# An mLSTM layer with two dense layers behind it on one core: leaky relu twice on ScalarE, its remainder read from the bank, the weights' integer addition on VectorE, and new durations in the planner

## The chip, the cores and the metric

The kernel runs on one core of one Trainium2 chip. The metric is the device time of one execution in microseconds; before the change the median of three runs is 894.95 us (892.51 to 896.52). In the text PE is TensorE, DVE is VectorE, ACT is ScalarE, POOL is GpSimd and SP is SyncE, whose queue issues every DMA of this kernel. A "bank" is one 128x512 float32 buffer of PSUM.

## The reference

Inputs are q, k, v and an output gate of shape (4, 8, 768, 40), two gates per head and token, and float64 weights of two dense layers. The recurrence runs over 768 tokens; its output, 3072 tokens by 320 columns, goes through two dense layers with 2048 hidden columns.

```python
for t in range(S):
    m_new = np.maximum(f_gate[:, :, t] + m, i_gate[:, :, t])
    f_stab = np.exp(f_gate[:, :, t] + m - m_new)
    i_stab = np.exp(i_gate[:, :, t] - m_new)
    C = f_stab * C + i_stab * einsum(v_t, k_t)
    n = f_stab * n + i_stab * k_t
    y[:, :, t] = sigmoid(o_t) * (C q_t) / max(abs(n q_t), 1)
x = y.transpose(0, 2, 1, 3).reshape(B * S, H * D)
h = x @ w_in;   x = np.maximum(0.01 * h, h) @ w_out        # layer 0
h = np.maximum(x @ w_in2, 0.0);   out = (h * h) @ w_out2   # layer 1
```

## The kernel before

**Tiling.** The recurrence is cut into six chunks of 128 tokens. A block is the same chunk of all four batches, 512 tokens, and each layer handles six blocks of 16 hidden tiles of 128 columns. To keep float32 accuracy a product is split into high and low float32r parts: `moe_h` writes a hidden tile with 8 matmuls into one of two banks named hp (line 424), `out1` (lines 454 to 460) adds 8 matmuls per tile into three accumulator banks in layer 0, and `out2` (lines 502 to 504) does the same with 12 shorter matmuls in layer 1. Block 0 of layer 0 is worked in halves of 256 tokens, because its tiles can only start as the weights come in; all other blocks go 512 tokens at a time. Attention of chunk 2 to 5 runs beside blocks 1 to 4 of layer 0, and attention of chunk 1 beside block 0.

**From a hidden tile to its two parts, layer 0.** The tile in the bank hp goes through four instructions: ACT copies it times 0.01 into g (line 430), DVE takes the maximum of g and the bank (line 431), ACT rounds that to the high part gH (line 435), and g minus gH is the low part gL (line 436), on DVE, or in block 0 also on POOL. The bank is free again after line 431.

**Weights.** A piece of weights comes as 704 float64 numbers per partition. DVE shifts and masks the high word (line 384) and merges it (line 386), ACT scales the low word (line 388), POOL adds the two as integers (line 389), ACT rounds the sum to the high parts (line 391), and the low parts are subtracted on DVE or POOL (lines 395 and 400). There are 16 pieces per layer; those of layer 0 are converted during start-up and block 0, those of layer 1 from block 4 of layer 0 on.

**What sets the order.** The program's order on every engine is written by a list scheduler, the class `Sched`. Each operation has an engine, a duration in ns, a priority, and the buffers that it reads and writes; an operation with `alt` may go to a second engine if the plan finds it free earlier. The scheduler runs the plan forward, works back from it to new priorities, and keeps the best of six passes. While the plan has PE idle in the first microseconds it puts in matmuls on zeros (lines 312, 450, 467), called fillers below. On the chip each engine runs its list strictly in order and waits by semaphores. Durations come from small functions such as

```python
def mm(n, m=128):                 # one pass of a float32r product
    return max(m / 1.2, n / 2.4 + 2.5, 25)
def dve(n, two_x=False):
    return (n / (2 if two_x else 1) + 66) / 0.96
```

**DMA.** SP issues all transfers in the planned order. The split queries and keys of a chunk are spread over partitions by nine transfers per batch, `T<-X` (line 569), after a rounding on ACT (line 564) and a subtraction on DVE (line 565); the products of line 623 wait for them.

Of the kernel before, what the change touches and what calls it, by code (L numbers as in the profile page):

```python
# [30 lines left out]
ORDER = dict(pe0=7000, ld2=80, kv=-5.41, ks=6.4, g2=32.54, z=-8.14, lag=7, m0=0.71, o0=1.33, a04=-6.78, a0s=5.39, a1=30.61, a1s=6.5, a1ld=23.83, w0=-23.81, ws=2.43, bias=0.88, c0=-7.4, cs=11.88, cld=28.29, wl=1.51, outk=2.04)  # L31
PASSES = 6                # of the list scheduler
# [6 lines left out]
class Buf:  # L39
    def __init__(self, tag, make):  # L40
        self.tag, self.make, self.t = tag, make, None
        self.first, self.left, self.last_w, self.readers, self.live = None, 0, {}, {}, tag is None


class Node:
    __slots__ = ("eng", "dur", "fn", "key", "deps", "outs", "ndep", "ready", "allocs", "bufs", "end", "start", "table", "lat", "seq", "alt", "after", "first")


class Sched:
# [10 lines left out]
    def op(self, eng, dur, key, fn, r=(), w=(), table=None, lat=0, alt=None, after=0):  # L60
        """fn() emits; r and w are the (buffer, region) pairs that it reads and writes; alt: another
        engine that may take it instead, with its time and fn."""
# [22 lines left out]
        n.bufs = list(bufs.values())  # L85
        n.deps = list(deps.values())
# [5 lines left out]
    def order(self, passes):  # L92
        """The best of some passes; each after the first takes its priorities from the one before: when an
        operation has to start for TensorE's operations to keep their order and to follow one another."""
        import copy

        best = None
        for i in range(passes):
            try:
                plan, total = self.forward()  # L100
            except RuntimeError:
                if best is None:
                    raise
                break
            if best is None or total < best[1]:
                best = [copy.copy(n) for n in plan], total
            self.backward(plan, total)
        return best[0]

    def backward(self, plan, total):  # L110
# [5 lines left out]
        for n in sorted((n for n in plan if n.seq >= 0), key=lambda n: (n.start, n.seq), reverse=True):  # L116
# [8 lines left out]
            if n.eng == "PE":            # the latest free time  # L125
# [8 lines left out]
    def forward(self):  # L134
# [103 lines left out]
def mm(n, m=128):                 # one pass of a float32r product  # L238
    return max(m / 1.2, n / 2.4 + 2.5, 25)
# [15 lines left out]
def mlstm_moe_kernel(  # L255
# [70 lines left out]
    def gate_part(lo, hi, key):  # L326
# [11 lines left out]
        op("DVE", dve(n), key, lambda: V.tensor_tensor_scan(m1(), f(), i(), NEG if lo == 0 else mt.t[:, lo:lo + 1], ALU.add, ALU.max),  # L338
# [11 lines left out]
        op("DVE", dve(n), key, lambda: V.tensor_tensor_scan(f(), am.t[:, 1, o], a(), 0.0, ALU.mult, ALU.add), r=[AA, (am, "mask")], w=[F])  # L350
# [5 lines left out]
        if lo:  # L356
            op("SP", 570, key + 0.1, lambda: SP.dma_start(out=Adram.t[:, o], in_=G_sb.t[32:64, o]), r=[(G_sb, f"A{p}")], w=[(Adram, p)], lat=500)
# [5 lines left out]
    wt, fs = {}, {}  # L363

    def weight(layer, j, key):
# [11 lines left out]
        op("SP", 570, key - 20, lambda: SP.dma_start(out=raw.t, in_=wts[layer, j].bitcast(I32).rearrange("p (n w) -> p n w", w=2)), w=[(raw, 0)], lat=2200)  # L377
# [11 lines left out]
        op("POOL", pool(WR), key, lambda: G.tensor_tensor(out=ft(), in0=ft(), in1=l.t, op=ALU.add), r=[(fb, fr), (l, 0)], w=[(fb, fr)])  # L389
# [7 lines left out]
        # the last 64 rows of w_in: its high parts in partitions 0..63, its low parts in 64..127  # L397
# [41 lines left out]

    def out1(c, lo, n, j, key):  # L440
# [7 lines left out]
        if j == 0 and n < BLK and lo == 0:      # one group of the whole bank for both halves  # L448
# [41 lines left out]
    def out2(c, j, key):  # L490
# [5 lines left out]
        for b in range(B):  # L496
# [10 lines left out]
            if last:  # L507
# [335 lines left out]
```

## Time and profile before

| quantity | value |
|---|---|
| three runs | 892.51, 896.52, 894.95 us; median 894.95 |
| profiled execution | span 888.7 us from the first to the last instruction; its time as a run is not listed beside it |
| busy in the span | PE 849.6, DVE 593.7, ACT 472.6, POOL 181.8 us |
| mean granted clock of TensorE | 0.975 |
| end of block 0 of layer 0 (line 472) | 167.1 us |
| ends of blocks 1, 2, 3 | 246.0, 325.9, 407.6 us |
| end of layer 0 | 541.5 us |

Busy shares are means over stages with different limits, so the stages are read apart below. The span is 6.3 us below the median of the runs, and differences are carried over to the median as they are.

### The profile page before, as it was taken

The page shows a single profiled execution, that of the slowest core. Times are in us where ns is not written, and L with a number is a line of the kernel's source. Part 1 is how long each engine was busy: PE and PEld are TensorE (multiplying, and loading weights), DVE is VectorE, ACT ScalarE, POOL GpSimd, SP SyncE. Part 2 cuts the span into 40 slices and gives each one's busy share as a digit, 9 for nine tenths or more (in the row PEclk, how much of TensorE's full clock was granted, in tenths as well). Part 3 has the DMA queues.
Part 4 walks back from the last instruction along what each step waited for, and adds up shares of the span by engine and source line. Part 5 has one row for each costly group of instructions (what it writes and reads, how often), then busy time and mean ns, then how long its engine had stood idle before and what let it go on. Part 6 is the DMA issues. An engine that isn't in the chain of part 4 may idle for free.

```text
span 888.7 us, 14153 instructions
## 1 busy us (share of the span) xinstructions
PE 849.6 (96%) x5244; PEld 732.1 (82%) x5244; DVE 593.7 (67%) x1047; ACT 472.6 (53%) x946; POOL 181.8 (20%) x190
## 2 busy tenths in 40 slices
PE   7988789999999999999999999999999999999998
PEld 5777789877777777777777888889999999999997
DVE  6699996877787778776867789964353443433433
ACT  5457665964775496558546556543343433433332
POOL 3387771511322042001000332200000000000000
PEclk8589899999999999999999999999999999999999
DMA  8477445434533444443331333200000000000000
GB/s 226 151 237 235 140 143 176 157 113 128 157 123 125 129 140 138 134 156 107 87 116 33 127 116 112 71 1 30 1 30 1 1 30 1 23 8 1 30 1 30
DMA packets 55992, 83.62 MB, mean 94 GB/s; under 512 B 4756, under 2 KB 44404, under 8 KB 55924
## 3 DMA queue, kind: packets, MB, share of 16 engines
q1 hardware_dynamic: 55924, 82.73, 29.2%
q8 instruction: 41, 0.67, 0.3%
q14 instruction: 27, 0.22, 0.1%
HBM read 54.43 MB, written 4.01 MB: 66 GB/s over the span
## 4 chain that ended last, share of the span: by engine, by line
PE 58%; DVE 17%; SPq 9%; DMA 6%; ACT 4%; issue 3%; POOL 3%; DVEq 0%; POOLq 0%; ACTq 0%
PE hp L424 25%; SPq L569 8%; DMA T<-X 4%; PE acc L503 3%; PE acc L504 3%; PE acc L502 3%; POOL qkr L389 2%; DVE gL L436 2%; PE acc L454 2%; DVE w L395 2%; PE acc L456 2%; PE acc L455 2%; PE attS L623 2%; PE atty L633 1%; DVE g L431 1%
## 5 line engine op out<-in xcount | busy, mean ns | idle before, releaser
L424 PE MATMUL hp<-xH,w 128*128 128x512 f32 (+1 forms) x1040 | 297.2, 383 | 8.1 <-DVE g L431 6.4
L424 PEld LDWEIGHTS hp<-xH,w 128*128 128x128 f32 x1040 | 185.8, 192 | 37.9 <-DVE g L431 7.1
L424 PE MATMUL hp<-xL,w 128*128 128x512 f32 (+1 forms) x624 | 201.4, 379 | 0.0
L436 DVE TENSOR_TENSOR gL<-g,gH 128x512 fp32r<-128x512 f32 (+1 forms) x196 | 143.3, 732 | 68.5 <-ACT gH L435 68.2
L435 ACT CAST gH<-g 128x512 fp32r<-128x512 f32 (+1 forms) x208 | 121.9, 586 | 124.6 <-DVE g L434 73.7
L434 DVE TENSOR_TENSOR g<-g 128x512 f32<-128x512 f32 x96 | 72.9, 759 | 114.2 <-ACT g L433 114.2
L424 PEld LDWEIGHTS hp<-xL,w 128*128 128x128 f32 x624 | 116.6, 191 | 22.9
L433 ACT ACTIVATE g<-hp 128x512 f32<-128x512 f32 x96 | 57.4, 598 | 122.4 <-PE hp L424 122.4
L431 DVE TENSOR_TENSOR g<-g,hp 128x512 f32<-128x512 f32 (+1 forms) x112 | 67.6, 605 | 29.9 <-ACT g L430 28.6
L456 PE MATMUL acc<-gL,w 128*128 128x512 f32 (+1 forms) x224 | 82.2, 367 | 4.7 <-DVE gL L436 2.4
L430 ACT ACTIVATE g<-hp 128x512 f32<-128x512 f32 (+1 forms) x112 | 59.7, 534 | 49.3 <-PE hp L424 41.2
L454 PE MATMUL acc<-gH,w 128*128 128x512 f32 (+1 forms) x224 | 85.9, 384 | 0.0
L455 PE MATMUL acc<-gH,w 128*128 128x512 f32 (+1 forms) x224 | 81.3, 363 | 0.0
L617 POOL TENSOR_SCALAR_AFFINE_SELECT aw<-aw 128x512 f32<-128x512 f32 x48 | 36.1, 754 | 118.2 <-ACT aw L614 117.8
L503 PE MATMUL acc<-w,gH 128*128 128x320 f32 x192 | 59.4, 309 | 0.0
L504 PE MATMUL acc<-w,gL 128*128 128x320 f32 x192 | 59.3, 309 | 0.0
L502 PE MATMUL acc<-w,gH 128*128 128x320 f32 x192 | 59.2, 308 | 0.0
L614 ACT ACTIVATE aw<-aw,cs 128x128 f32<-128x128 f32 x160 | 51.1, 392 | 5.0 <-DMA aw<-Adram 4.9
L456 PEld LDWEIGHTS acc<-gL,w 128*128 128x128 f32 x224 | 42.9, 192 | 12.6 <-POOL gL L436 2.7
L389 POOL TENSOR_TENSOR qkr<-qkr,wl 128x704 int32<-128x704 int32 x16 | 30.5, 1909 | 100.1 <-DVE qkr L386 60.6
L455 PEld LDWEIGHTS acc<-gH,w 128*128 128x128 f32 x224 | 43.1, 192 | 5.7
L454 PEld LDWEIGHTS acc<-gH,w 128*128 128x128 f32 x224 | 43.2, 193 | 5.4
(162 smaller groups left out, 1569.9 us busy)
## 6 DMA issues: line engine op xcount, KB each, us to landing
T<-X SPq DMA_DIRECT2D x180, 120.0 KB
x<-in_wts_dram SPq DMA_DIRECT2D x16, 704.0 KB
aw<-Adram SPq DMA_DIRECT2D x40, 256.0 KB
nat<-in_nat_dram SPq DMA_DIRECT2D x24, 328.0 KB
qkr<-in_qk_dram SPq DMA_DIRECT2D x20, 360.0 KB
X<-in_wts_dram SPq DMA_DIRECT2D x8, 704.0 KB
T<-in_wts_dram SPq DMA_DIRECT2D x8, 704.0 KB
og<-in_og_dram SPq DMA_DIRECT2D x12, 320.0 KB
```

Source lines behind the costliest of these rows:

```text
L424: T.matmul(hp.t[:, 0:n], w.t[:, col:col + 128], x.t[:, kt, o], start=(s == 0), stop=(s == 7))
L431: op("DVE", dve(n), key, lambda: V.tensor_tensor(out=g.t[:, 0:n], in0=g.t[:, 0:n], in1=hp.t[:, 0:n], op=ALU.max), r=[(hp, 0), (g, 0)], w=[ ...
L434: op("DVE", dve(n), key, lambda: V.tensor_tensor(out=g.t[:, 0:n], in0=g.t[:, 0:n], in1=g.t[:, 0:n], op=ALU.mult), r=[(g, 0)], w=[(g, 0)])
L435: op("ACT", act(n), key, lambda: A.copy(gH.t[:, 0:n], g.t[:, 0:n]), r=[(g, 0)], w=[(gH, 0)])
L436: lo_ = lambda eng: eng.tensor_tensor(out=gL.t[:, 0:n], in0=g.t[:, 0:n], in1=gH.t[:, 0:n].bitcast(F32), op=ALU.subtract)
L454: T.matmul(a[t].t[:, o], w.t[:, hc:hc + 128], gH.t[:, 0:n], start=first, stop=False)
L455: T.matmul(a[t].t[:, o], w.t[:, lc:lc + 128], gH.t[:, 0:n], start=False, stop=False)
L456: T.matmul(a[t].t[:, o], w.t[:, hc:hc + 128], gL.t[:, 0:n], start=False, stop=last)
L502: T.matmul(a.t[:, 0:DM], gH.t[:, s], wH, start=first, stop=False)
L503: T.matmul(a.t[:, 0:DM], gH.t[:, s], wL, start=False, stop=False)
L504: T.matmul(a.t[:, 0:DM], gL.t[:, s], wH, start=False, stop=last)
L569: op("SP", 570, kx, lambda tt=tt, X=X, blk=blk, r=r, x0=x0, x1=x1: SP.dma_start(out=tt.t[blk * D:(blk + 1) * D, :, r].bitcast(F32), in_=X. ...
```

## The change

The comments were also taken out of the file, so that line numbers shift by 7 to 9 (line 430 becomes 438, 436 becomes 440, 389 becomes 396).

```diff
         if layer == 0:
-            op("ACT", act(n, True), key, lambda: A.activation(g.t[:, 0:n], hp.t[:, 0:n], AF.Copy, scale=0.01), r=[(hp, 0)], w=[(g, 0)])
-            op("DVE", dve(n), key, lambda: V.tensor_tensor(out=g.t[:, 0:n], in0=g.t[:, 0:n], in1=hp.t[:, 0:n], op=ALU.max), r=[(hp, 0), (g, 0)], w=[(g, 0)])
+            h = lambda: hp.t[:, 0:n]
+            op("ACT", act(n, True), key, lambda: A.activation(gH.t[:, 0:n], h(), AF.Prelu, alpha=0.01), r=[(hp, 0)], w=[(gH, 0)])
+            op("ACT", act(n, True), key, lambda: A.activation(h(), h(), AF.Prelu, alpha=0.01), r=[(hp, 0)], w=[(hp, 0)])
+            op("DVE", dve(n), key, lambda: V.tensor_tensor(out=gL.t[:, 0:n], in0=h(), in1=gH.t[:, 0:n].bitcast(F32), op=ALU.subtract), r=[(hp, 0), (gH, 0)], w=[(gL, 0)])
...
-        op("ACT", act(n), key, lambda: A.copy(gH.t[:, 0:n], g.t[:, 0:n]), r=[(g, 0)], w=[(gH, 0)])
-        lo_ = lambda eng: eng.tensor_tensor(out=gL.t[:, 0:n], in0=g.t[:, 0:n], in1=gH.t[:, 0:n].bitcast(F32), op=ALU.subtract)
-        op("DVE", dve(n), key, lambda: lo_(V), r=[(g, 0), (gH, 0)], w=[(gL, 0)], alt=("POOL", pool(n), lambda: lo_(G)) if n < BLK else None)
...
-        op("POOL", pool(WR), key, lambda: G.tensor_tensor(out=ft(), in0=ft(), in1=l.t, op=ALU.add), r=[(fb, fr), (l, 0)], w=[(fb, fr)])
+        add = lambda eng: eng.tensor_tensor(out=ft(), in0=ft(), in1=l.t, op=ALU.add)
+        op("DVE", dve(WR), key, lambda: add(V), r=[(fb, fr), (l, 0)], w=[(fb, fr)], alt=("POOL", pool(WR), lambda: add(G)))
...
-def mm(n, m=128):
-    return max(m / 1.2, n / 2.4 + 2.5, 25)
+def mm(n):
+    return max(112, 0.4427 * n + 5.6)
...
+                b = busy[{"DVE": "POOL", "POOL": "DVE"}.get(e)] if e in ("DVE", "POOL") else None
+                if b and not n.bank and not b.bank:
+                    dur += SHARE * min(dur, max(0, b.start + b.dur - now))
```

With `SHARE = 0.6` the plan lengthens an operation of DVE or POOL that starts while the other of the two is busy, unless one of them touches a bank (`n.bank`). Other durations in the plan change as well: a DMA issue from 570 to 420 ns, and to 800 for the transfers `T<-X` and the copies of the state; the two scans of the gates, the transposes, and the small products of attention. The priorities in the table `ORDER` stay as they were. In layer 1 the four instructions per tile stay.

Since the plan changes, the order changes on all engines; three places follow. The first is DVE at the start, behind the first part of the gates. `T`, `x_0` and `x_1` belong to the gates' scans, `x_2` and `x_4` to the first piece of weights, and `aw` times `attS` is the first product of attention, which PE waits for. Before:

```order
L338 SCALAR_TENSOR_TENSOR T<-x_0_73,T 32x128
L340 TENSOR_TENSOR x_1_82<-x_0_73,T 32x128
L338 SCALAR_TENSOR_TENSOR T<-x_0_73,T 32x512
L341 TENSOR_TENSOR x_1_82<-x_1_82,T 32x128
L340 TENSOR_TENSOR x_1_82<-x_0_73,T 32x512
L349 TENSOR_TENSOR x_0_73<-x_0_73,T 32x512
L341 TENSOR_TENSOR x_1_82<-x_1_82,T 32x512
L344 TENSOR_SCALAR x_1_82<-x_1_82 32x128
L344 TENSOR_SCALAR x_1_82<-x_1_82 32x512
L349 TENSOR_TENSOR x_0_73<-x_0_73,T 32x128
L626 TENSOR_TENSOR aw<-aw,attS 128x512
```

Now:

```order
L345 SCALAR_TENSOR_TENSOR T<-x_0_73,T 32x128
L635 TENSOR_TENSOR aw<-aw,attS 128x512
L635 TENSOR_TENSOR aw<-aw,acc_163 128x512
L345 SCALAR_TENSOR_TENSOR T<-x_0_73,T 32x512
L391 TENSOR_SCALAR x_2_226<-x_4_125 128x704
L347 TENSOR_TENSOR x_1_82<-x_0_73,T 32x512
```

The two products moved ahead of nine gate operations. On SP the second load of the gates, for which the first of these rows waits, stands tenth instead of seventh.

The second place is in block 0, one or two pieces of weights on DVE, around the eighth piece. Before:

```order
L384 TENSOR_SCALAR x_2_254<-x_4_586 128x704
L565 TENSOR_TENSOR X<-qkr,X 120x2x384
L386 SCALAR_TENSOR_TENSOR x_2_254<-x_4_586,x_2_254 128x704
L740 TENSOR_TENSOR xL<-attm,xH 128x3x128
L431 TENSOR_TENSOR g<-g,hp 128x256
L626 TENSOR_TENSOR aw<-aw,attS 128x512
L384 TENSOR_SCALAR x_3_278<-x_5_636 128x704
L431 TENSOR_TENSOR g<-g,hp 128x256
L386 SCALAR_TENSOR_TENSOR x_3_278<-x_5_636,x_3_278 128x704
L395 TENSOR_TENSOR w_878<-x_2_254,w_878 128x512
```

Now:

```order
L391 TENSOR_SCALAR x_2_226<-x_4_657 128x704
L440 TENSOR_TENSOR gL<-hp,gH 128x256
L393 SCALAR_TENSOR_TENSOR x_2_226<-x_4_657,x_2_226 128x704
L635 TENSOR_TENSOR aw<-aw,attS 128x512
L749 TENSOR_TENSOR xL<-attm,xH 128x3x128
L396 ISA x_2_226<-x_2_226,wl 128x1408
L391 TENSOR_SCALAR x_3_354<-x_5_667 128x704
L440 TENSOR_TENSOR gL<-hp,gH 128x256
L393 SCALAR_TENSOR_TENSOR x_3_354<-x_5_667,x_3_354 128x704
L403 TENSOR_TENSOR w_880<-x_2_226,w_880 128x512
```

The maximum (L431) is gone, the remainder (L440) has its place and reads the bank, and the integer addition (L396) has come in as an instruction of its own kind whose row speaks of 1408 elements. Of the 16 additions of layer 0, ten are on DVE and six on POOL; of layer 1's, fifteen and one. All 32 remainders of half tiles are on DVE (before 20, and 12 on POOL). Of the 16 small subtractions of line 400 (now 408) in layer 0 none is on DVE (before four), and of the 512-wide ones of line 395 (now 403) thirteen are (before fifteen).

The third place is ACT in a later block of layer 0. Before:

```order
L430 ACTIVATE g<-hp 128x512
L657 CAST x_5_1933<-aw 128x512
L435 CAST gH<-g 128x512
L729 COPY y<-y 128x64
L430 ACTIVATE g<-hp 128x512
L739 CAST xH<-attm 128x3x128
L435 CAST gH<-g 128x512
```

Now:

```order
L438 ACTIVATE gH<-hp 128x512
L738 COPY y<-y 128x64
L439 ACTIVATE hp<-hp 128x512
L748 CAST xH<-attm 128x3x128
L438 ACTIVATE gH<-hp 128x512
L439 ACTIVATE hp<-hp 128x512
```

Each tile still has two ACT instructions, and both now read the bank; the second writes it. The number of table loads on ACT is the same in both programs. Of the fillers, fifteen of line 467 (now 476) stand in the order instead of ten, and as many as before of the two other lines.

## Rows read from the trace of the kernel before

**Rows 1.** Windows by stage: us, busy (instructions) per engine, granted clock, DMA.

```profile
0.00:44.00 44.00, 38.34 (x207) 29.53 (x208) 28.43 (x63) 21.40 (x49) 14.89 (x22) 0.69 0.62 189
44.00:133.00 89.00, 73.23 (x597) 69.09 (x596) 85.11 (x142) 57.40 (x133) 68.13 (x68) 0.90 0.59 188
133.00:167.00 34.00, 33.37 (x293) 31.51 (x292) 24.44 (x56) 22.98 (x56) 10.69 (x14) 1.00 0.59 176
167.00:541.50 374.50, 361.06 (x2250) 291.96 (x2249) 290.99 (x549) 236.79 (x483) 75.82 (x81) 1.00 0.38 121
541.50:888.70 347.20, 343.60 (x1905) 309.97 (x1903) 164.77 (x242) 134.07 (x228) 12.23 (x7) 1.00 0.06 20
```

**Rows 2.** Groups of DVE, 44 to 133 us: count, busy us, mean ns, idle before.

```profile
L386 DVE SCALAR_TENSOR_TENSOR x<-x,x 128x704 int32<-128x704 int32 x13 | 13.6, 1043 | 0.1
L395 DVE TENSOR_TENSOR w<-x,w 128x512 fp32r<-128x512 f32 x13 | 12.7, 974 | 0.1
L384 DVE TENSOR_SCALAR x<-x 128x704 int32<-128x704 int32 x12 | 10.3, 865 | 0.0
L436 DVE TENSOR_TENSOR gL<-g,gH 128x256 fp32r<-128x256 f32 x12 | 9.5, 806 | 0.5 <-ACT gH L435 0.5
L431 DVE TENSOR_TENSOR g<-g,hp 128x256 f32<-128x256 f32 x23 | 9.3, 412 | 0.5 <-ACT g L430 0.3
L400 DVE TENSOR_TENSOR w<-x,w 64x128 fp32r<-64x128 f32 x3 | 4.6, 1530 | 0.1
```

**Rows 3.** The same lines over the whole span: ns shortest/median/longest, starts, forms.

```profile
L386 DVE SCALAR_TENSOR_TENSOR x<-x,x x16: 874/884/1941, 25.2 to 122.4; 128x704 int32<-128x704 int32 x16
L395 DVE TENSOR_TENSOR w<-x,w x15: 676/834/2079, 34.5 to 127.7; 128x512 fp32r<-128x512 f32 x15
L384 DVE TENSOR_SCALAR x<-x x16: 511/522/1985, 22.3 to 120.4; 128x704 int32<-128x704 int32 x16
L436 DVE TENSOR_TENSOR gL<-g,gH x196: 409/692/1908, 55.1 to 881.0; 128x512 fp32r<-128x512 f32 x176, 128x256 fp32r<-128x256 f32 x20
L400 DVE TENSOR_TENSOR w<-x,w x4: 289/504/3581, 36.3 to 104.7; 64x128 fp32r<-64x128 f32 x4
```

**Rows 4.** Timeline of DVE and POOL around 96 us: start, length, what.

```profile
95.99 3.58 DVE L400 TENSOR_TENSOR w<-x,w 64x128 fp32r<-64x128 f32 x1
...
96.50 1.29 POOL L395 TENSOR_TENSOR w<-x,w 128x512 fp32r<-128x512 f32 x1
97.76 1.66 POOL L389 TENSOR_TENSOR x<-x,wl 128x704 int32<-128x704 int32 x1
```

**Rows 5.** Groups of POOL, 44 to 133 us.

```profile
L389 POOL TENSOR_TENSOR x<-x,wl 128x704 int32<-128x704 int32 x14 | 26.7, 1909 | 7.8 <-DVE x L386 7.7
L436 POOL TENSOR_TENSOR gL<-g,gH 128x256 fp32r<-128x256 f32 x10 | 11.5, 1147 | 2.2 <-ACT gH L435 2.0
L400 POOL TENSOR_TENSOR w<-x,w 64x128 fp32r<-64x128 f32 x11 | 8.1, 737 | 4.8 <-ACT w L391 2.3 <-issue 1.4 <-POOL aw L617 0.5
```

**Rows 6.** Waits of PE, 44 to 133 us, by releaser: us, times, longest.

```profile
PE hp L424 <- DVE g L431: 6.4, 2, 3.9
```

**Rows 7.** The line of ACT's first instruction per hidden tile, layer 0.

```profile
L430 ACT ACTIVATE g<-hp x112: 360/592/603, 48.5 to 533.4; 128x512 f32<-128x512 f32 x80, 128x256 f32<-128x256 f32 x32
```

**Rows 8.** Windows at the start, columns as in rows 1.

```profile
12.50:17.00 4.50, 0.18 (x2) 0.00 (x0) 4.50 (x10) 4.18 (x5) 1.52 (x2) 0.72 0.89 291
17.00:41.50 24.50, 24.41 (x118) 19.40 (x120) 16.26 (x34) 11.47 (x32) 10.07 (x11) 0.50 0.51 167
```

**Rows 9.** Groups of DVE, 167 to 541 us.

```profile
L436 DVE TENSOR_TENSOR gL<-g,gH 128x512 fp32r<-128x512 f32 x81 | 62.5, 772 | 10.5 <-ACT gH L435 10.4
L431 DVE TENSOR_TENSOR g<-g,hp 128x512 f32<-128x512 f32 x79 | 53.9, 682 | 26.3 <-ACT g L430 25.4
```

**Rows 10.** Waits of PE, 167 to 541 us.

```profile
PE attS L623 <- DMA T<-X: 8.3, 15, 0.7
```

**Rows 11.** SP's issues of those transfers.

```profile
L569 SPq DMA_DIRECT2D T<-X x180: 767/768/1244, 49.9 to 451.9; - x180
```

More of the change, by code (lines that the diff above doesn't have):

```diff
@@ L31 @@
 ORDER = dict(pe0=7000, ld2=80, kv=-5.41, ks=6.4, g2=32.54, z=-8.14, lag=7, m0=0.71, o0=1.33, a04=-6.78, a0s=5.39, a1=30.61, a1s=6.5, a1ld=23.83, w0=-23.81, ws=2.43, bias=0.88, c0=-7.4, cs=11.88, cld=28.29, wl=1.51, outk=2.04)
+SHARE = 0.6
 PASSES = 6
@@ L42, in __init__ @@
         self.first, self.left, self.last_w, self.readers, self.live = None, 0, {}, {}, tag is None
+        self.bank = False
 class Node:
-    __slots__ = ("eng", "dur", "fn", "key", "deps", "outs", "ndep", "ready", "allocs", "bufs", "end", "start", "table", "lat", "seq", "alt", "after", "first")
+    __slots__ = ("eng", "dur", "fn", "key", "deps", "outs", "ndep", "ready", "allocs", "bufs", "end", "start", "table", "lat", "seq", "alt", "after", "first", "bank")
 class Sched:
@@ L85, in op @@
         n.bufs = list(bufs.values())
+        n.bank = any(b.bank for b in n.bufs)
         n.deps = list(deps.values())
@@ L282, in ps @@
         b = sc.buf(tag, None, 2 if tag == "hp" else 1)
+        b.bank = True
         b.make = lambda: pp.tile([128, 512], F32, tag=tag, name=tag, bufs=sc.slots[tag])
@@ L301, in mlstm_moe_kernel @@
     for lo, hi in ((0, CH), (CH, S)):
-        op("SP", 570, -1000, lambda lo=lo, hi=hi: SP.dma_start(out=fi.t[:, :, lo:hi], in_=gates[:, :, lo:hi].rearrange("g p s -> p g s")),
+        op("SP", 420, -1000, lambda lo=lo, hi=hi: SP.dma_start(out=fi.t[:, :, lo:hi], in_=gates[:, :, lo:hi].rearrange("g p s -> p g s")),
            w=[(fi, f"{x}{p}") for x in "fi" for p in ((0,) if lo == 0 else (1, 2))], lat=250)
@@ L337, in gate_part @@
         ck = lambda x: x.rearrange("p (k t) -> p k t", t=CH)
-        op("DVE", dve(n), key, lambda: V.tensor_tensor_scan(m1(), f(), i(), NEG if lo == 0 else mt.t[:, lo:lo + 1], ALU.add, ALU.max),
+        op("DVE", 3.4 * n, key, lambda: V.tensor_tensor_scan(m1(), f(), i(), NEG if lo == 0 else mt.t[:, lo:lo + 1], ALU.add, ALU.max),
            r=[F, I, (mt, p)], w=[(mt, p + 1)])
@@ L349, in gate_part @@
         op("DVE", dve(n), key + 0.1, lambda: V.tensor_tensor(out=i(), in0=i(), in1=m1(), op=ALU.subtract), r=[I, (mt, p + 1)], w=[I])
-        op("DVE", dve(n), key, lambda: V.tensor_tensor_scan(f(), am.t[:, 1, o], a(), 0.0, ALU.mult, ALU.add), r=[AA, (am, "mask")], w=[F])
+        op("DVE", 2.2 * n + 60, key, lambda: V.tensor_tensor_scan(f(), am.t[:, 1, o], a(), 0.0, ALU.mult, ALU.add), r=[AA, (am, "mask")], w=[F])
         op("DVE", dve(n, True), key, lambda: V.tensor_copy(G_sb.t[32:64, o], f()), r=[F], w=[(G_sb, f"A{p}")])
@@ L376, in weight @@
         wt[layer, j] = w
-        op("SP", 570, key - 20, lambda: SP.dma_start(out=raw.t, in_=wts[layer, j].bitcast(I32).rearrange("p (n w) -> p n w", w=2)), w=[(raw, 0)], lat=2200)
+        op("SP", 420, key - 20, lambda: SP.dma_start(out=raw.t, in_=wts[layer, j].bitcast(I32).rearrange("p (n w) -> p n w", w=2)), w=[(raw, 0)], lat=2200)
         l = sb("wl", [128, WR], I32, 2)
@@ L633, in mI @@
                             T.matmul(py.t[:, (8 + n) * E:(9 + n) * E], lhs(0, h), st, start=True, stop=True)
-                    op("PE", 4 * (214 if native else 107), key + 0.35, mI, r=tk + ([(C32, (b, 0)), (C32, (b, 1))] if native else [(Cst, (b, k)) for k in range(3)]), w=[(py, 0)])
+                    op("PE", 4 * (214 if native else 113), key + 0.35, mI, r=tk + ([(C32, (b, 0)), (C32, (b, 1))] if native else [(Cst, (b, k)) for k in range(3)]), w=[(py, 0)])
                 def mPV(py=py, aw=aw, v=v, hd=hd):
@@ L659, in attention @@
                        alt=("POOL", pool(512), lambda lw=lw: lw(G, 1)))
-                    op("PE", 4 * 145, key + 0.5, mPV3, r=[(pb, (pr, i)) for i in range(3)] + [(vb, (vr, i)) for i in range(3)], w=[(py, 0)])
+                    op("PE", 4 * 126, key + 0.5, mPV3, r=[(pb, (pr, i)) for i in range(3)] + [(vb, (vr, i)) for i in range(3)], w=[(py, 0)])
                 else:
@@ L693, in mU @@
                         T.matmul(up.t[r:r + D, o:o + E], nt.t[:, h * D:(h + 1) * D], wv.t[:, h], start=True, stop=True)
-                op("PE", 8 * 62, kU, mU, r=[(nt, 0), (wv, 0)], w=[(up, 0)])
+                op("PE", 730, kU, mU, r=[(nt, 0), (wv, 0)], w=[(up, 0)])
                 st = lambda b=b: C32.t[:, 8 * b:8 * b + 8]
@@ L734, in mT @@
                     T.transpose(xp.t[:, k * 128:(k + 1) * 128], y.t[:, k * 128:(k + 1) * 128], ident.t)
[L736 removed]
+            op("PE", 3 * 112, ko + 0.75, mT, r=[(y, 0), (y, 1), (ident, 0)], w=[(xp, 0)])
             xo = slice(b * CH, (b + 1) * CH)
```

33 lines of the change are left out of this document (17 added, 16 removed).

## Prediction

> **What bounds the kernel now.** I read the windows by stage first. In layer 1, the last 347 us, PE is busy 99% of the time at full clock [rows 1]; the change leaves its four instructions per tile as they are, so nothing is to be had there. Blocks 1 to 5 of layer 0 (167 to 541.5 us) have PE busy 361.1 of 374.5 us: 13.4 us idle. The stage to look at is 44 to 133 us, start of block 0: PE is busy only 73.2 of 89 us and gets a mean clock of 0.90, while DVE is busy 85.1 us, 96%, and POOL 68.1 us, 77%. DVE is the bound there. It converts the weights, serves attention and the hidden tiles, and the PE waits that are left in that stretch come from it, as the 6.4 us for line 431 do [rows 6]. From 133 to 167 us PE catches up, 98% busy.
>
> Second, what DVE does in that stretch. Its groups are longer than they need be: line 386 takes 1043 ns in the mean where its shortest takes 874, line 395 974 against 676, line 384 865 against 511, line 436 806 against 409, line 400 1530 against 289 [rows 2, 3]. Line 431 with 412 ns is not stretched: half of its input comes from a bank. The timeline shows how the others are. One subtraction of 64x128 elements on DVE starts at 95.99 us and lasts 3.58 us, 12 times its shortest, and ends when two POOL operations that started beside it have ended, at 97.79 and 99.42 us [rows 3, 4]. Summed over the five lines (13 x 169, 13 x 298, 12 x 354, 12 x 397 and 3 x 1241 ns) this stretching is 2.2 + 3.9 + 4.2 + 4.8 + 3.7 = 18.8 us.
>
> [...]
>
> **The change part by part.** The sum is made against the profiled span of 888.7 us, 6.3 us under the median of the runs, and carried to the median, 894.95.
>
> *Block 0, DVE's own work at shortest durations.* Removed: 32 maxima of half tiles at 0.412 = 13.2 us, and 20 remainders that DVE had at 0.409 = 8.2 us; four small subtractions and two wide ones go to POOL, 4 x 0.289 + 2 x 0.676 = 2.5 us. Added: 32 remainders that read the bank, the form of line 431, 32 x 0.412 = 13.2 us; and ten integer additions. No row shows such an addition on DVE. Below, I take line 384, which goes over the same 704 words with one source, 0.51 us; above, twice line 386, since the order speaks of 1408 elements, 1.75 us. I take line 386 itself, 0.88 us, nearest because it has the same tile and two sources: 8.8 us, between 5.1 and 17.5. Sum: -13.2 - 8.2 - 2.5 + 13.2 + 8.8 = -1.9 us [rows 2, 3].
>
> [...]
>
> *Block 0, the stretching.* The 4.8 us of line 436 go, since the remainder now reads the bank. The other 14.0 us I scale with POOL's load in the stretch: ten of its additions leave, 10 x 1.909 = 19.1 us, and its ten remainders, 11.5 us; four small and two wide subtractions arrive, 4 x 0.737 + 2 x 1.29 = 5.5 us [rows 4, 5]. That is 25.1 of 68.1 us, 37%, so 5.2 us. The additions on DVE will be stretched themselves; at line 386's 0.17 us each that gives back 1.7 us. Net -8.3 us. Between nothing (what remains of POOL still hits DVE as often) and -18.8.
>
> So DVE's queue is 10.2 us shorter up to the end of block 0. PE has 15.8 us of idleness there, plus what the clock of 0.90 costs, so it can take the weights that much earlier. I count 9 us, a little less, because the tail from 133 us is PE's own.
>
> *ACT.* Two instructions per tile before and after, the second now on the bank instead of a rounding. Line 430 reads the same bank in 592 ns for 512 columns [rows 7]; I price both at that, the in-place one included, between the 360 ns of a half tile's shortest and twice 603. ACT is busy 57.4 of 89 us in the stretch and 236.8 of 374.5 later [rows 1], so up to 0.3 us more on each is hidden behind DVE and PE. The number of table loads is equal in both orders. Cost 0.
>
> *Start.* The first two products of attention move ahead of nine gate operations on DVE. Before, PE idled from 12.5 to 17 us for them and then ran at half clock to 41.5 us [rows 8]. Against that, the second part of the gates is loaded three issues later, and five more fillers stand in PE's list. I take 0, between -8 and +4.
>
> *Blocks 1 to 5.* DVE loses 79 maxima of 0.682, 53.9 us, and each remainder falls from 0.772 to 0.682 [rows 9]; ten or so additions for layer 1 bring 9 us. DVE wasn't the bound, PE has only 13.4 us of idleness [rows 1]. Of it 8.3 us are waits for the transfers `T<-X`, 15 times up to 0.7 us [rows 10]. Each of the nine issues takes 0.768 us of SP, which the old plan booked at 0.57 and the new one at 0.8 [rows 11]: nine now start 2 us earlier in the plan, more than the longest wait. I take -6, between 0 and -13.4.
>
> *Layer 1.* 0: PE is 99% busy. Of its weights' additions 15 of 16 go to DVE, which has time.
>
> Sum: -9 + 0 + 0 - 6 + 0 = -15 us: a span of 874 and a median of **880 us**.
>
> **Rivals.** *The addition costs 1.75 us (forecast's weak term).* Ten of them add 8.7 us to DVE in its bound stage, and the block 0 gain is nearly gone: -6 in all, 889 us. For it: the 1408 elements. Against: the one-source line 384 already passes over 704 words in 0.51 us.
>
> *The bank becomes the round trip.* Before, a bank of hp is free after ACT and the maximum on DVE. Now it waits for ACT, ACT again, and a remainder that stands in DVE's queue behind weights. With two banks and a DVE that is full, PE then waits in block 0 on every half tile: 32 times 0.38, the second ACT pass at line 430's length for a half tile (0.36 to 0.4), is 12 us in place of the 9 gained, so 880 + 9 + 12 = 901 us, slower. It decides if DVE stays above 95% busy while PE comes to a half tile every 3.8 us, as it did (32 in the 123 us from 44 to 167). For it: the only long PE waits in the stretch are already for the bank, 6.4 us in two waits [rows 6]. Against: only two, in 32 half tiles.
>
> *The clock rises early.* If the earlier product keeps PE from idling, the 24.5 us at half clock shorten; PE's 24.4 busy us would take 12.2, but DVE has 16.3 us of work in them [rows 8], so at most 8 us: 872 us.
>
> *The change doesn't reach the end.* The plan is new on every engine while the priorities are the old ones; what DVE gains could be lost in a worse order elsewhere: 895 us, give or take 4.
>
> **How the numbers follow.** 0.5%, 4.5 us, is about what a measurement of this kernel tells from no change. Forecast 0.55 (own range 870 to 887); dear addition 0.14, two thirds of it still faster; bank 0.11; early clock 0.10; no effect 0.10. Faster 0.55 + 0.09 + 0.10 = 0.74, same 0.05 + 0.10 = 0.15, slower 0.11. The range takes in all but the bank rival and a little below the clock rival, where both gains add to a cheap addition: 865 to 896.
>
> **What would show it.** Right: POOL busy some 43 us instead of 68 in the like stretch, lines 391, 393 and 403 nearer to 511, 874 and 676 ns, the remainder of half tiles near 412 ns, line 396 on DVE at 0.88 us, line 472's counterpart first at about 158 us instead of 167, and PE idle between 167 us and the end of layer 0 cut by half. Wrong: line 396 above 1.5 us; PE waiting for the remainder (line 440) before line 432 in dozens of places; a first copy of block 0's result at 167 us or later; blocks 1 to 5 still at 374 us.

## The result and the profile after

The changed kernel takes **880.35 us** in the median of four runs (878.64 to 881.54), the kernel before 894.12 beside it: a ratio of 0.984 (0.982 to 0.987). Six more runs of the same program gave 878.96 us and 0.984 (0.980 to 0.988). Runs more than 1.5% above the fastest of their kernel are left out of the medians and ratios of the experiments below, and since the profiles of old_plan and tx_800 are of such runs, only the T<-X waits are read from them.

The profiled execution took 881.54 us with a span of 879.8, that is 8.9 us less than the profiled span of before, while the medians lie 14 us apart: the profiled executions of before lie near the low end of its runs, which go from 887.83 to 899.92 us (the second took 889.98 us, below). Windows of the changed kernel with the cuts of [rows 1]; columns as there:

```profile
0.00:44.00 44.00, 39.48 (x222) 31.04 (x223) 22.47 (x53) 20.45 (x51) 12.51 (x20) 0.73 0.51 143
44.00:133.00 89.00, 76.35 (x629) 70.94 (x629) 83.09 (x155) 60.61 (x144) 50.45 (x54) 0.94 0.71 220
133.00:167.00 34.00, 32.69 (x257) 30.43 (x256) 18.23 (x39) 20.29 (x48) 7.84 (x11) 0.90 0.51 162
167.00:541.50 374.50, 368.11 (x2288) 295.64 (x2288) 269.96 (x513) 241.91 (x493) 45.43 (x58) 1.00 0.39 126
```

POOL fell from 68.1 to 50.5 us in the stretch 44 to 133, DVE only from 85.1 to 83.1: its queue was not emptied, it came earlier. PE's idleness from 167 to 541.5 us fell by half, from 13.4 to 6.4 us.

The rows of single lines say what the new instructions cost: count, then shortest/median/longest in ns.

```profile
L396 DVE CUSTOM_DVE_ANT_0 qkr<-qkr,wl x15: 873/891/895, 468.1 to 553.3; 128x1408 uint16<-128x1408 uint16 x15
L396 DVE CUSTOM_DVE_ANT_0 x<-x,wl x10: 872/1008/2394, 43.1 to 116.2; 128x1408 uint16<-128x1408 uint16 x10
L396 POOL TENSOR_TENSOR x<-x,wl x6: 1675/1826/2177, 24.2 to 115.9; 128x704 int32<-128x704 int32 x6
L440 DVE TENSOR_TENSOR gL<-hp,gH x112: 374/683/692, 49.5 to 528.7; 128x512 fp32r<-128x512 f32 x80, 128x256 fp32r<-128x256 f32 x32
L439 ACT ACTIVATE hp<-hp x112: 358/588/608, 48.4 to 527.4; 128x512 f32<-128x512 f32 x80, 128x256 f32<-128x256 f32 x32
L578 SPq DMA_DIRECT2D T<-X x180: 767/768/1476, 54.3 to 449.3; - x180
```

The addition on DVE costs 0.87 us at the shortest, the remainder that reads the bank 0.68 us as line 431 did, the leaky relu in place on the bank 0.59 us, no more than line 430's [rows 7]. Among layer 1's pieces, from 468 us on, where POOL is busy only 2.9 of 86 us, all fifteen additions lie within 22 ns; in block 0 the longest is 2.39 us. Groups of DVE in the stretch 44 to 133 us, columns as in [rows 2]:

```profile
L393 DVE SCALAR_TENSOR_TENSOR x<-x,x 128x704 int32<-128x704 int32 x14 | 14.8, 1056 | 0.0
L396 DVE CUSTOM_DVE_ANT_0 x<-x,wl 128x1408 uint16<-128x1408 uint16 x10 | 11.6, 1164 | 0.0
L403 DVE TENSOR_TENSOR w<-x,w 128x512 fp32r<-128x512 f32 x13 | 10.2, 788 | 2.1 <-ACT w L399 2.1
L440 DVE TENSOR_TENSOR gL<-hp,gH 128x256 fp32r<-128x256 f32 x24 | 9.9, 413 | 1.2 <-ACT hp L439 1.0
L391 DVE TENSOR_SCALAR x<-x 128x704 int32<-128x704 int32 x14 | 9.4, 682 | 0.3 <-DMA x<-in_wts_dram 0.3
```

And the waits of PE over the whole span: releaser, us in all, times, longest.

```profile
PE attS L544 <- DVE aw L635: 5.1, 1, 5.1
PE hp L432 <- DVE gL L440: 4.8, 5, 2.7
PE atty L648 <- DVE aw L635: 3.9, 2, 3.1
PE atty L656 <- DVE x L662: 2.5, 5, 0.9
PE hp L432 <- ACT xH L748: 1.5, 1, 1.5
PE hp L319 <- DVE xL L316: 1.3, 1, 1.3
PE attS L632 <- DMA T<-X: 1.2, 2, 0.6
```

The `T<-X` waits, fifteen of 8.3 us together in blocks 1 to 5 before [rows 10], are down to two, both in block 0. The largest wait is new and single: 5.1 us in front of line 544. The copy that closes a block starts at 165.3 us for block 0 (before 167.1) and at 533.3 for block 5 (541.5): block 0 gained 1.8 us, blocks 1 to 5 took 368.0 us instead of 374.4, the rest 346.5 instead of 347.2. In the second profile of the changed kernel block 0 ends at 159.7 us and blocks 1 to 5 take 369.0; its first 44 us and its blocks 1 to 5:

```profile
0.00:44.00 44.00, 40.19 (x273) 30.68 (x273) 27.93 (x64) 23.38 (x58) 17.88 (x24) 0.88 0.62 182
159.70:528.70 369.00, 361.75 (x2253) 290.19 (x2252) 261.56 (x503) 237.26 (x488) 44.13 (x57) 1.00 0.40 127
```

### The profile page after: what moved, and what is told of

Same layout as the page of the kernel before. It is cut to its first block, busy times and chain, and to the rows that moved or that the text cites. A ratio compares the mean times of both kernels' runs of the same rounds, so it can differ in the third digit from the quotient of the medians.

```text
span 879.8 us, 13999 instructions
## 1 busy us (share of the span) xinstructions
PE 851.7 (97%) x5249; PEld 730.7 (83%) x5249; DVE 543.3 (62%) x982; ACT 468.7 (53%) x946; POOL 116.2 (13%) x143
## 4 chain that ended last, share of the span: by engine, by line
PE 74%; DVE 7%; SPq 6%; DMA 5%; ACT 4%; issue 2%; POOL 0%; ACTq 0%; DVEq 0%
PE hp L432 34%; SPq L578 6%; PE acc L463 3%; PE acc L512 3%; PE acc L513 3%; PE acc L511 3%; PE acc L465 3%; PE acc L464 3%; PE acc L468 2%; PE attS L632 2%; PE acc L469 2%; DMA T<-X 2%; PE atty L642 1%; PE atty L648 1%; DMA x<-in_gates_dram 1%
## 5 line engine op out<-in xcount | busy, mean ns | idle before, releaser
L444 DVE TENSOR_TENSOR g<-g 128x512 f32<-128x512 f32 x96 | 66.6, 694 | 116.2 <-ACT g L443 116.2
L443 ACT ACTIVATE g<-hp 128x512 f32<-128x512 f32 x96 | 57.3, 597 | 128.7 <-PE hp L432 128.7
L446 DVE TENSOR_TENSOR gL<-g,gH 128x512 fp32r<-128x512 f32 x96 | 67.6, 704 | 56.4 <-ACT gH L445 56.4
L445 ACT CAST gH<-g 128x512 fp32r<-128x512 f32 x96 | 59.5, 620 | 67.7 <-DVE g L444 67.7
L440 DVE TENSOR_TENSOR gL<-hp,gH 128x512 fp32r<-128x512 f32 (+1 forms) x112 | 68.0, 609 | 37.8 <-ACT hp L439 37.3
L438 ACT ACTIVATE gH<-hp 128x512 fp32r<-128x512 f32 (+1 forms) x112 | 59.6, 532 | 58.4 <-PE hp L432 54.9
L439 ACT ACTIVATE hp<-hp 128x512 f32<-128x512 f32 (+1 forms) x112 | 59.2, 528 | 0.1
L626 POOL TENSOR_SCALAR_AFFINE_SELECT aw<-aw 128x512 f32<-128x512 f32 x48 | 33.2, 692 | 171.2 <-ACT aw L623 146.9
```

The lines of the kernel that those rows point to most:

```text
L438: op("ACT", act(n, True), key, lambda: A.activation(gH.t[:, 0:n], h(), AF.Prelu, alpha=0.01), r=[(hp, 0)], w=[(gH, 0)])
L440: op("DVE", dve(n), key, lambda: V.tensor_tensor(out=gL.t[:, 0:n], in0=h(), in1=gH.t[:, 0:n].bitcast(F32), op=ALU.subtract), r=[(hp, 0), ( ...
L444: op("DVE", dve(n), key, lambda: V.tensor_tensor(out=g.t, in0=g.t, in1=g.t, op=ALU.mult), r=[(g, 0)], w=[(g, 0)])
L445: op("ACT", act(n), key, lambda: A.copy(gH.t, g.t), r=[(g, 0)], w=[(gH, 0)])
L446: op("DVE", dve(n), key, lambda: V.tensor_tensor(out=gL.t, in0=g.t, in1=gH.t.bitcast(F32), op=ALU.subtract), r=[(g, 0), (gH, 0)], w=[(gL, 0)])
```

## The experiments

Three parts can be taken apart: the leaky relu, the addition, the planner's durations. The kernels below are the eight corners of that cube, then one figure of the planner by itself, then one row moved. In the table T<-X is what PE waits for these transfers from 167 to 541 us (rows with that releaser), "engines" what it waits there for DVE, ACT and POOL together, and blocks 1 to 5 run from the first to the last closing copy.

| kernel | leaky | add | planner | us, median | ratio (95%) | T<-X | engines | blocks 1–5 |
|---|---|---|---|---|---|---|---|---|
| before | – | – | old | 894 | 1 | 9.2 | 2.2 | 374.4 |
| plan_only | – | – | new | 896.99 | 1.003 (1.001–1.006) | 0 | 10.4 | 374.0 |
| relu_only | new | – | old | 891.17 | 0.999 (0.997–1.001) | 8.1 | 0.8 | 385.2 |
| add_only | – | new | old | 888.12 | 0.996 (0.993–0.999) | 8.9 | 3.5 | 376.5 |
| old_plan | new | new | old | 887.72 | 0.993 (0.989–0.996) | 7.5 | – | – |
| no_add | new | – | new | 884.19 | 0.989 (0.986–0.993) | 0 | 8.0 | 372.2 |
| no_relu | – | new | new | 887.32 | 0.992 (0.988–0.996) | 0 | 9.7 | 374.7 |
| changed | new | new | new | 878.96 | 0.984 (0.980–0.988) | 0 | 6.0 | 368.0 |
| tx_570 | new | new | new, T<-X old | 899.45 | 1.006 (1.003–1.009) | 8.0 | 7.8 | 386.1 |
| tx_800 | new | new | old, T<-X new | 884.36 | 0.991 (0.988–0.994) | 0 | – | – |
| before_800 | – | – | old, T<-X new | 912.96 | 1.021 (1.018–1.023) | 0 | 24.5 | 401.9 |
| s_early | new | new | new, a row moved | 878.55 | 0.984 (0.981–0.986) | 0 | 5.4 | 366.0 |

In the row of the changed kernel the time is that of its six later runs, the waits and blocks are those of its first profile; the second has 6.3 and 369.0. A closing copy is that of the first of three accumulators. In relu_only and before_800 the third is copied 8 us later at the end of block 0 (in before 0.6), so 385.2 and 401.9 hold work of block 0; from third copy to third copy it is 381.1 and 396.8 us, in before 376.8.

**One part alone (plan_only, relu_only, add_only), and both engine edits under the old plan (old_plan).** The theories on record: A, two gains that add up (freed DVE in block 0, better placed transfers later); B, all of it from DVE's freed time; C, any new order of the program moves the total by some microseconds through single long waits. The edits, of which plan_only has the first hunk alone, relu_only and add_only the second or third, old_plan both of them without the first:

```diff
-def mm(n, m=128): return max(m / 1.2, n / 2.4 + 2.5, 25)
+def mm(n): return max(112, 0.4427 * n + 5.6)
-op("SP", 570, kx, lambda tt=tt, X=X, ...
+op("SP", 800, kx, lambda tt=tt, X=X, ...
...
@@
-A.activation(g.t, hp.t, AF.Copy, scale=0.01); V.tensor_tensor(g.t, g.t, hp.t, op=ALU.max); A.copy(gH.t, g.t); gL = g - gH
+A.activation(gH.t, h(), AF.Prelu, alpha=0.01); A.activation(h(), h(), AF.Prelu, alpha=0.01); gL = hp - gH
@@
-op("POOL", pool(WR), key, lambda: G.tensor_tensor(out=ft(), in0=ft(), in1=l.t, op=ALU.add), ...)
+op("DVE", dve(WR), key, lambda: add(V), ..., alt=("POOL", pool(WR), lambda: add(G)))
```

> The kernel before with the planner's new durations and nothing else. Theory A (two separate gains: freed VectorE time in block 0, better placed transfers in blocks 1 to 5): block 0 still ends near 167 us, blocks 1 to 5 take 368 us instead of 374, PE's waits for the T<-X transfers fall from 9.2 us to under 3; median 888 against 894. Theory B (all of it is VectorE's freed time): no difference, 893 to 895, and the waits for T<-X stay at 8 us or more. Theory C (any new order moves the total by some us either way): a total off by 3 us or more, with no relation to those waits.

> Only the leaky relu twice on ScalarE with the remainder from the bank; addition on GpSimd and the planner's durations as before. Theory A: the last piece of weights of layer 0 is ready some 5 us earlier than 128.4 us, blocks 1 to 5 still take 373 to 375 us; median 889. Theory B: it carries most of the gain, blocks 1 to 5 near 368 us; 883 to 885. Theory C: a total that fits neither, with a new long wait of PE in block 0.

> Only the integer addition on VectorE or GpSimd, by the plan's choice; the rest as before. Theory A: VectorE's queue in block 0 grows by ten or more additions of 0.88 us and loses about 5 us of stretching, so the last piece is ready within 3 us of 128.4 us; median 892 to 896. Theory B: a gain of 3 us or more. Theory C: a total off by more than 3 us either way that comes from one or two long waits of PE.

> The change without the planner's new durations: leaky relu and addition as changed, durations and the sharing rule as before. Theory A: blocks 1 to 5 back at 372 to 374 us with T<-X waits near 9 us, block 0 as in the change or better; median 886. Theory B: the same as the change, 879 to 882. Theory C: more than 4 us away from both, by a wait in block 0.

No part alone brings the gain: by the ratios +0.3%, -0.1% and -0.4%, together -1.6%. Two kernels missed what A said of them: add_only gained more (888.1, where A had 892 to 896 and B a gain of 3 us or more), and the blocks of relu_only took longer than 373 to 375 us. B falls with old_plan, which has all of DVE's relief and gains 0.7%; A's simple sum falls with plan_only, which was to bring the gain of blocks 1 to 5 and is slower than before. The waits of plan_only from 167 to 541 us show why; its four largest:

```profile
PE attm L742 <- DVE y L735: 3.7, 3, 1.7
PE atty L641 <- DVE hs L682: 2.8, 5, 1.1
PE attm L701 <- DVE xL L748: 1.1, 2, 0.8
PE hp L432 <- ACT xH L747: 0.9, 1, 0.9
```

Not one T<-X row is left, but products now wait 10.4 us for engines, DVE above all, where they waited 2.2 before. The blocks take 374.0 us, as before. This made theory D, two doors behind one another: the transfers are the first, DVE the second, and opening one hands the time to the other.

**The missing corners, and one figure put back.** The edits to the changed kernel: none (after_again); the addition back on POOL (no_add); the old leaky relu (no_relu); and tx_570:

```diff
-                        op("SP", 800, kx, lambda tt=tt, X=X, ... 
+                        op("SP", 570, kx, lambda tt=tt, X=X, ...
```

> The changed kernel once more, beside the others of this batch. Theory D (two doors): blocks 1 to 5 lose some 8 us to products that wait for the T<-X transfers as long as the planner counts an issue on SP shorter than it is, and, once that is mended, 6 to 8 us to products that wait for VectorE as long as VectorE does the old leaky relu; each repair alone hands the time to the other wait, both together gain about 10 us. It expects 880 here, blocks 1 to 5 at 368, T<-X waits under 2 us in the stretch 167 to 541 us. Theory C (order luck: any new order of the program moves the total by some 5 us, and this is a good one) expects 880 as well, since it is the same order. Both expect block 0 to end between 157 and 167 by where the half clock falls in this execution.

> The change with the weights' integer addition left on POOL (new planner durations and new leaky relu stay). Theory D: T<-X waits under 2 us, VectorE waits in the stretch 167 to 541 us near the 6 us of the full change or a little above, since the leaky relu was the larger part there; blocks 1 to 5 at 368 to 371, total 880 to 886. Theory C: a new order, total anywhere between 880 and 897, with no tie to the T<-X waits.

> The change with the old leaky relu (copy, maximum and remainder from memory) and the other two parts. Theory D: no T<-X waits, but products wait for VectorE some 9 to 11 us in the stretch 167 to 541 us as with the planner's durations alone; blocks 1 to 5 at 372 to 375, total 887 to 893. Theory C: total anywhere between 880 and 897.

> The full change with one planner figure put back: an issue of the T<-X transfers counted as 570 ns instead of 800. Theory D: the T<-X waits come back, 7 to 9 us in the stretch 167 to 541 us as before the change; blocks 1 to 5 at 374 to 377, total 886 to 891. Theory C: total anywhere between 876 and 892, and the T<-X waits need not come back, since thirty other durations of the planner are still new. If the waits come back and the total stays at 880, they are not what the time hangs on.

The totals of the first three came out as D has them (878.96, 884.19, 887.32; only the blocks of no_add, 372.2 us, lie 1 us above its 368 to 371), with no T<-X wait from 167 to 541 us and the engines' waits larger the less DVE is relieved: 6.0, 8.0 and 9.7 us. By the medians, across the two batches (before took 893.7 and 893.8 in them), the leaky relu is worth 2.6 us under the old plan and 12.8 under the new one (plan_only 897.0 to no_add 884.2); the planner costs 3 us alone and brings 9 on top of both edits (old_plan 887.7 to 879.0). With tx_570 the transfers' waits came back, as many times as before [rows 10]; its four largest waits from 167 to 541 us:

```profile
PE attS L632 <- DMA T<-X: 8.0, 15, 0.7
PE attS L632 <- ACT ex L549: 3.5, 3, 1.3
PE atty L656 <- DVE x L662: 2.7, 4, 0.9
PE attS L632 <- issue: 1.5, 3, 0.7
```

But the total is 899.5 us, 8 to 13 more than D said. The stretch of its blocks 1 to 5:

```profile
168.90:555.00 386.10, 368.61 (x2253) 296.61 (x2252) 256.55 (x500) 233.84 (x487) 43.67 (x61) 0.98 0.38 121
```

PE idles 17.5 of 386.1 us, 11 more than in the changed kernel, and the granted clock is 0.98 instead of 1.00. By an estimate from these figures, with 0.50 as the lower clock as in [rows 8], PE is at it for 2 x 0.02 x 386 = 15 us, and its work lasts up to 8 us longer. With the 11 us of idleness that accounts for the 18 us that these blocks lost. That the waits hang on this figure was expected; that this order also comes with a lower clock was not. Its trace shows where: from 194 to 196 us two short waits, 0.57 and 0.72 us, leave PE busy 0.80 of 2 us, and in the next 2 us stretches the clock is 0.67 and 0.50. The same follows two more such pairs, at 258 and 362 us. In before a pair of such waits, 1.2 us together at 416 us, left the clock at 1.00; why the one order loses its clock at them and the other does not is not shown.

**The same figure alone, on two kernels (tx_800, before_800), and one row of DVE moved (s_early).** tx_800 is old_plan, before_800 the kernel before, both with 570 made 800 in that one line. s_early takes the product of line 635 for the last group of chunk 0 out of the finished order and puts it right behind what it depends on:

```diff
+        m = product[0, 7]
+        n = plan.pop(at[m.seq])
+        plan.insert(max(at[d.seq] for d in m.deps) + 1, n)
```

On DVE it is the only row that moves, ahead of seven others. This is the place in the changed kernel (timeline of DVE with one row each of POOL and PE, other rows left out; start, length, what, and idle time before):

```profile
55.21 0.96 DVE L391 TENSOR_SCALAR x<-x 128x704 int32<-128x704 int32 x2 [0.33 <-DMA x<-in_wts_dram]
56.09 0.88 DVE L393 SCALAR_TENSOR_TENSOR x<-x,x 128x704 int32<-128x704 int32 x1
56.89 0.89 DVE L396 CUSTOM_DVE_ANT_0 x<-x,wl 128x1408 uint16<-128x1408 uint16 x1
57.12 2.18 POOL L396 TENSOR_TENSOR x<-x,wl 128x704 int32<-128x704 int32 x1 [2.30 <-DVE x L393]
57.69 2.35 DVE L393 SCALAR_TENSOR_TENSOR x<-x,x 128x704 int32<-128x704 int32 x1
59.97 0.67 DVE L635 TENSOR_TENSOR aw<-aw,attS 128x512 f32<-128x512 f32 x1
60.70 0.42 PE L544 MATMUL attS<-ident,G_sb 96*128 96x96 f32 x1 [5.14 <-DVE aw L635]
```

> The new leaky relu and the new addition under the old planner durations, with one of the new ones: an issue of the T<-X transfers counted as 800 ns instead of 570. Theory D (two doors): this figure is what the planner's part is worth, so the T<-X waits fall under 2 us in the stretch 167 to 541 us, blocks 1 to 5 take 368 to 372 us and the total is 878 to 885, as with the full change. Rival P (all of the planner's durations are needed): T<-X waits partly gone, total 886 to 891, near the same two edits under the old durations alone (890). Order luck (C): 876 to 892 with no tie to the waits.

> The kernel before with that one figure alone (T<-X issue 800 instead of 570), no other edit. Theory D: the T<-X waits go, and waits for VectorE take their place in the stretch 167 to 541 us (8 to 11 us, as with all the planner's durations alone); blocks 1 to 5 at 372 to 376, total 889 to 897. Rival: if the T<-X waits alone were the loss, blocks 1 to 5 fall to 366 to 368 and the total to 884 to 887.

> The changed kernel with one row of VectorE moved ahead: the product of the attention weights with S for the last group of chunk 0 goes in front of the five weight operations behind which it stood. Theory W (that row's place costs block 0 the time): TensorE's wait for it, 5.1 and 3.4 us in the two profiles of the changed kernel, falls under 1 us, block 0 ends 3 to 6 us earlier than the 160 to 165 us seen so far, total 873 to 877. Rival: TensorE has nothing to do behind it before the next weights are ready (their transfer landed at 55.2 us), so the wait moves to the first hidden product behind it and the total stays at 878 to 881.

tx_800 has no T<-X waits and lands at the upper edge of D (884.4). But on top of both edits this figure brings only 3 of the 9 us that the planner's part brings, and the intervals of old_plan (0.989 to 0.996) and tx_800 (0.988 to 0.994) overlap nearly whole: a gain of this figure alone is not shown. The other durations bring more, 5 us, so D was too simple and P has a share. before_800 goes D's way and beyond: no T<-X wait, and 19 us slower than before. Its largest waits from 167 to 541 us, and windows around one of them:

```profile
PE attm L742 <- DVE y L735: 17.6, 5, 4.8
PE attm L701 <- DVE xL L748: 2.7, 2, 1.3
```

```profile
238.00:242.00 4.00, 1.95 (x23) 1.35 (x22) 3.93 (x8) 3.26 (x9) 4.00 (x6) 0.90 0.24 82
242.00:246.00 4.00, 0.90 (x3) 0.51 (x3) 2.73 (x8) 1.48 (x5) 1.22 (x2) 0.50 0.45 152
246.00:250.00 4.00, 3.00 (x21) 2.48 (x22) 1.50 (x4) 0.26 (x1) 0.00 (x0) 0.50 0.81 255
```

A product that waits 4.8 us for DVE's `y`, behind block 1's end at 237.5 us, leaves PE busy 2.85 of 8 us, and the clock is at half (0.50 from 242 to 250 us, after 1.00 up to 238) behind it. So in this trace the wait is paid twice, with its own length and with the half clock behind it, where the fifteen short ones of [rows 10] were paid once: blocks 1 to 5 of before had a clock of 1.00. Those of tx_570 were not all so cheap.

In s_early the wait is gone, block 0 ends at 162.6 us, between the 165.3 and 159.7 of the changed kernel, and the total is unchanged (878.55 against 878.96). Its largest wait is now

```profile
PE hp L432 <- ACT w L399: 5.6, 1, 5.6
```

PE waits for the next converted weight instead, until 62.6 us: theory W falls, and the rival is right that the wait only moves. What holds that weight shows in the chain of waits of this kernel (start, length, what):

```profile
55.65 0.81 DVE x L393
...
56.60 2.99 POOL x L396
...
59.62 0.03 ACT wl L395
...
60.35 0.76 ACT w L399
61.11 0.74 ACT wl L395
61.85 0.67 ACT w L399
```

It is not the transfer but an integer addition that the planner left on POOL, 2.99 us long beside DVE's work. ACT's next line 395 waits for its end. Behind that in ACT's queue come the rounding of another weight, which DVE's own addition had finished by 57.3 us (line 399, at 60.35), one more line 395, and only then, at 61.85 us, the rounding for which PE waits: by the program's order that of the weight whose addition POOL did. A version with these early additions all on DVE was not tried.

**The kernel before, profiled again (before_again).**

> The kernel before, profiled a second time, for where its time lies. The change's gain by the medians is 14 us, of which blocks 1 to 5 hold 5 to 6 and layer 1 under 1 in the profiles, so some 7 should lie in block 0: by that block 0 ends at 167 to 171 us here (the changed kernel's two profiles end it at 165.3 and 159.7), blocks 1 to 5 take 373 to 376, the T<-X waits are 7 to 9 us in the stretch 167 to 541 us, and the total is 890 to 896. Rival (block 0 only scatters between executions and gained nothing): it ends at 158 to 163 us here, and blocks 1 to 5 must be longer than 376 for a total of 890 to 896.

Block 0 ends at 166.9 us, a hair before the range given and well after that of the rival; blocks 1 to 5 take 374.2 us, with 8.5 us of T<-X waits from 167 to 541 us; the total is 889.98. The first profile of before is no accident.

## Why the prediction was right, and where it was not

**The total**, 880, was met to 0.4 us, but it is a sum of which one term was right, one half right, and whose carrying from the profiled span to the median helped. That it was met so closely is in part luck.

*Integer addition, 0.88 us.* Right: 872 ns at the shortest, 0.87 to 0.90 in layer 1. The rival of 1.75 us falls. The row of the addition on DVE has 128x1408 uint16 where POOL's has 128x704 int32, and line 386, which I took for its length, takes 874 ns at the shortest [rows 3].

*Stretching, -8.3 us.* Near. Against the shortest lengths of [rows 3] and the 872 ns of line 396, lines 391, 393, 396 and 403 lose 14 x 171 + 14 x 182 + 10 x 292 + 13 x 112 ns = 9.3 us from 44 to 133 us, where it was 18.8. But not by the even scaling I used: the two-source line 393 is stretched as before (1056 against 1043 ns), the additions by 0.29 us each rather than 0.17, and most of the gain comes from the small subtractions, all 15 of them now on POOL (3.7 us), and from the remainders (4.8 us), which read the bank and take 413 ns in the mean where line 436 took 806. Lines 391 and 403 lose 4.3 us less to stretching than before, and the additions' own stretching takes 2.9 us of that back. Why an operation of DVE lasts longer beside one of POOL is not shown.

*Block 0 ends 9 us earlier.* **This step failed**: "PE has 15.8 us of idleness there ... so it can take the weights that much earlier". DVE did its part: the last wide low part of a weight (line 403, before 395) is ready at 120.8 us, 7.6 earlier than the 128.4 of before. But block 0 closes only 1.8 us earlier. Windows from 44 us to that weight and from there to the block's end, before and after:

```profile
44.00:128.40 84.40, 69.50 (x554) 65.52 (x553) 80.71 (x132) 55.72 (x129) 64.52 (x64) 0.90 0.59 191
128.40:167.10 38.70, 37.20 (x336) 35.18 (x336) 28.95 (x66) 24.76 (x63) 14.30 (x19) 1.00 0.59 173
```

```profile
44.00:120.80 76.80, 64.46 (x518) 59.33 (x518) 73.38 (x132) 53.73 (x124) 47.32 (x49) 0.93 0.72 227
120.80:165.30 44.50, 42.87 (x360) 40.59 (x359) 27.58 (x63) 25.50 (x64) 10.34 (x16) 0.92 0.55 167
```

PE idles 1.5 and 1.6 us in the second windows: behind the last weight it is PE's work that counts. There are 24 more products to do there, 2.7 us at the 0.11 us that one of before's 336 took in the mean, and the clock is 0.92 instead of 1.00. That is 2 x 0.08 x 44.5 = 7 us at half clock (0.50 from 142 to 148 us), worth up to 3.6 us; it follows a wait of 0.8 us for line 635, near 140 us. By this estimate the two make up the 5.8 us by which the window is longer. Weights that come early find a queue. In relu_only it was the same: the last wide low part was ready at 115.0 us, 13 us earlier than in before, but the third accumulator was copied only 3 us earlier, at 164.4 us. Of PE's idleness from 44 us to the block's end, 16.4 us before, 14.0 us are left after and 12.9 in the second profile: 2.4 to 3.5 us came of it, and not 9. s_early shows one of the waits that remain: a weight that stands behind an addition on POOL.

*Start, 0, between -8 and +4.* Inside the bounds, and it scatters: clock 0.73 in the first 44 us of one profile and 0.88 in the other, against 0.69 before. By an estimate with 0.50 as the lower clock [rows 8], that is 2 x 0.27 and 2 x 0.12 of 44 us at half clock, 24 and 11 us. The difference of 13 us is worth up to 6.6 us; the second profile closes block 0 5.6 us earlier. What I gave as a rival, an early clock, happens in some executions. Both profiles of before have 0.69; whether the new order makes it likelier is not shown.

*Blocks 1 to 5, -6.* Right in size: -6.4 and -5.2 us. That the waits go with the issue counted as 800 instead of 570 is shown by the table: T<-X waits of 7.5 to 9.2 us in all five kernels with 570, none in the seven with 800. That their going alone is worth 6 us is not: on top of both edits the figure brought no clear gain (tx_800). But "DVE wasn't the bound" there is true only while the transfers hold PE up. Without the new leaky relu, plan_only and no_relu give the time back, above all in waits for DVE.

*ACT and the bank's round trip.* Right: line 439 costs what line 430 did, and PE waits for line 440 five times, 4.8 us in all, not at every half tile [rows 6]. The bank rival falls. *Layer 1*, 0: 346.5 against 347.2 us.

*The sum.* Measured on profiles it is -8.9 us (879.8 against 888.7) and -13.0 (875.3 against 888.3), where I had -15; by the medians -14 to -15. Why the two profiled executions of before lie 4 us under their median, when the changed kernel's first lies 1 us over its own, is open. So is how much of each total is luck of the order (theory C): tx_570 is slower by 8 to 13 us than its waits alone let expect. s_early, one moved row, left the total as it was, but no run has an order that differs more and leaves these waits alone.

## What to carry to other kernels

Where a planner orders the work, a transfer that it books too short can be paid as short waits: here fifteen of up to 0.7 us, 8.3 us in all, for issues booked at 570 ns that took 768 [rows 10, 11]. Measure the planner's durations and the engine edits together: each part alone was worth 0.4% or less here and the two engine edits 0.7%, the one figure alone cost 2.1% on the old kernel and brought no clear gain beside the engine edits, all durations with them gained 1.6%. When an engine that feeds TensorE gets faster, count only the idleness that TensorE has while it waits for it; of work that arrives earlier than TensorE can take it little is left: here the last wide low part was ready 7.6 us earlier, and block 0 closed 1.8 us earlier.

## What the runs showed that was not expected

- The price of a wait was not its length alone. In before fifteen waits of up to 0.7 us left the clock at 1.00 in blocks 1 to 5 [rows 1, 10]; in tx_570 fifteen of the same kind came with a clock of 0.98, some of the half clock right behind them. In before_800 five waits that sum to 17.6 us, the longest 4.8, came with a clock of 0.96 over 401.9 us, by the same estimate (2 x 0.04 x 401.9) 32 us of it at half.
- One and the same program scatters with the clock: the changed kernel's spans run from 873.1 us at a mean granted clock of 0.984 to 886.0 at 0.969, before's from 886.1 at 0.980 to 898.2 at 0.967. Two profiles can differ by more than the change is worth in a stage; block 0's end did, 165.3 against 159.7 us.
- The integer addition of line 396 stands in the trace of the changed kernel on DVE as a row of its own kind, 128x1408 uint16, at 872 ns at the shortest; on POOL as 128x704 int32, at 1675 ns at the shortest.
